# Statistics on ScalarE, a slab in halves and two more transforms by eight in a gated convolution kernel

## The chip, the cores and the metric

The kernel runs on one core of a Trainium2 chip. The metric is the device time of one execution in microseconds; before the change it is 1929.6 us, the median of three runs (1929.02 to 1932.13). A core has a matrix engine (TensorE, PE in the profile, with its weight loads as PEld), a vector engine (VectorE, DVE), an engine for functions of one operand (ScalarE, ACT), a general engine (GpSimd, POOL) and a queue engine (SyncE, SP). Each of them works through its own instructions in order and waits on semaphores for the others. SP, ACT and POOL also issue DMA transfers between the memory (HBM) and the core's own memory; TensorE writes its products into the banks of a small memory, PSUM, from which ScalarE and VectorE read.

## The reference

The reference computes a forward pass and all gradients of a block with two branches, for a sequence of S = 2048 rows and D = 1024 columns in bf16:

```python
xn = layernorm(x)                       # x = A_q
k_shift = causal convolution of k with 4 taps per column (A_shift_k)
kv = k_shift * v
y = irfft(rfft(kv, padded to 2S) * rfft(ssm_k, padded to 2S))[:S] + kv * ssm_D
s = xn * y
g = silu(((xn @ w_gate) * (xn @ w_up)) @ w_down)     # F = 3584
out = x + s * g
```

The outputs are out and the gradients of x, k, v, shift_k, ssm_k, ssm_D, w_gate, w_up and w_down, taken with a given grad_out.

## The kernel before

The rows are 16 blocks of 128. The first stage normalises them, turns them (transposes them 128 by 128 on TensorE) into the tiles XNT, and multiplies them with the gate and up weights. The weights come in 14 slabs of 256 columns of F. One unit (`gu_unit`, L629) takes one slab and 1, 2 or 4 blocks: for each block eight matmuls of 128x512 into a bank psg (L645, two banks), a cast to gut on ScalarE (L647) and a store of gut. The product of gate and up, hN, is one multiply on VectorE for the whole unit (L659). It is written one block later, into the order of the next unit. Five blocks after that TensorE turns hN (L674), ScalarE copies it, and it is stored for the down product.

The layer norm (`layer_norm`, L554) works on chunks of 1, 1, 2, 4, 4 and 4 blocks. For each block VectorE takes two `bn_stats` and a `bn_aggr`; for the chunk it casts the variances to var_b, adds epsilon (vpe, L566), ScalarE takes the root (half_r, L569), VectorE forms the reciprocal and normalises block by block (L580). The order of the loads on SP is: chunk 0, chunk 1, slab 0, chunk 2, slab 1, chunks 3 to 5 (L866 to L872).

The convolution (`conv_forward`, L685) works on eight groups of 128 columns, with Fourier transforms that are split: TensorE multiplies with small tables T4 (psF, L235), ScalarE copies the sums out (SP), and VectorE adds and subtracts them into the spectra. KX and HX are the spectra of the filter and of kv; `product` multiplies them; the inverse (`inv_dft` or `inv8` on VectorE, then psY on TensorE) gives y. Each transform has two forms. One does a split by four on VectorE (`fwd4_sums` and `fwd4_outs`, `inv_dft`) and leaves more matmuls; the other does a split by eight (`fwd8`, L297; `inv8`, L395) with half the matmuls and more VectorE instructions. The list `EIGHT` names the pairs of group and transform that take the second form, and `INV8` the groups whose inverse does. The shifted product of k with the taps (`shift`, L703) starts the convolution and comes again for every second group; it is not to start before the last normalisation (`last`, L710).

The order of convolution work beside the units is set by a pump: each block of a unit is a tick (`tick`, L918), and at each tick the pump emits convolution work until its share, in weights that stand at the yields, has come up to the share of ticks over `NT`. From the first transform on VectorE's instructions are pinned to the written order (`PIN`), and on each engine the order is fixed when the program is built. Before that point the order comes from a scheduler; `issue_after` keeps an instruction from being placed before another. The start of the stage also has: the turning of the last two chunks, put off to a later unit (`turn_late`, L602); the angles of the tables, made on POOL, masked on VectorE and turned into sines on ScalarE (L169 to L184); the first loads of k, v and the filter (A_ssm_k, into U5) on POOL.

After the units comes the down product (psbm, L971), with the gate and the gradients behind it. These later stages are not touched.

## Time and profile before

| what | us |
|---|---|
| median of three runs | 1929.6 |
| profiled execution | 1929.84 |
| its span, first to last instruction | 1928.1 |
| TensorE busy | 1914.2 |
| VectorE busy | 1542.1 |
| ScalarE busy | 638.8 |
| first forward convolution multiply on VectorE | 51.30 |
| first psbm matmul on TensorE | 519.0 |

The profiled execution's own time holds 1.7 us around the span. A line of a timeline gives the start, the length, engine, line, operation, tile written and read, shapes and count, and in brackets the idle time of the engine before it with what ended it. A line of waits gives the engine and tile that waited, for what, the sum, the number of times and the longest, in microseconds. A busy TensorE is not one at its peak, since the ends of its matmuls are modelled; the granted clock says how fast it ran.

### The profile page before, as it was taken

How to read it: one execution, taken by the hardware profiler on the slowest of the kernel's cores; microseconds unless marked ns; L12 is line 12 of the kernel's file. 1: busy time of each engine (PE TensorE's matmuls, PEld its weight loads, DVE VectorE, ACT ScalarE, POOL GpSimd, SP SyncE). 2: the span in 40 equal slices, each digit the busy share in tenths (PEclk: the TensorE clock that was granted, in tenths of full speed). 3: DMA queues.
4: the chain of work that ended last, by engine and by line, in shares of the span. 5: the costliest groups of instructions: out<-in, count | busy, mean ns of one | idle time of the engine just before them, and what ended most of it. 6: DMA issues, size and time to landing. Idle time of an engine off the chain costs nothing.

```text
span 1928.1 us, 27453 instructions
## 1 busy us (share of the span) xinstructions
PE 1914.2 (99%) x10978; PEld 1030.8 (53%) x10978; DVE 1542.1 (80%) x1695; ACT 638.8 (33%) x943; POOL 329.1 (17%) x461
## 2 busy tenths in 40 slices
PE   8999999999999999999999999999999999999999
PEld 5555655555444456665666666664444444444444
DVE  8999999999956555888799999999996403388884
ACT  5754655555332233343222222222222102011113
POOL 5121212201112210000122132021211101111111
PEclk9999999999999999999999999999999999999999
DMA  8776867659799988666788798585787999889984
GB/s 292 269 259 217 261 208 236 219 209 293 242 294 293 302 284 262 208 202 215 253 249 262 245 244 264 200 273 177 223 254 175 152 199 201 177 174 200 187 189 159
DMA packets 451360, 444.43 MB, mean 231 GB/s; under 512 B 268800, under 2 KB 371612, under 8 KB 436768
## 3 DMA queue, kind: packets, MB, share of 16 engines
q1 hardware_dynamic: 394848, 243.36, 47.7%
q0 software_dynamic: 40064, 169.95, 28.0%
q10 hardware_dynamic: 16320, 29.36, 4.1%
q8 instruction: 86, 1.41, 0.3%
q14 instruction: 42, 0.34, 0.1%
HBM read 194.00 MB, written 185.64 MB: 197 GB/s over the span
## 4 chain that ended last, share of the span: by engine, by line
PE 91%; DVE 6%; issue 1%; ACT 1%; DMA 0%; SPq 0%; ACTq 0%; DVEq 0%
PE psb L1344 20%; PE psx L1474 20%; PE psg L645 14%; PE psb L1327 10%; PE psbm L971 10%; PE psb L1422 9%; PE psF L235 3%; DVE W L213 2%; DVE HX L213 1%; PE tr L674 1%; PE psY L438 1%; DVE KX L213 1%; PE psY L1130 1%; PE psx L1422 1%; DVE U L213 1%
## 5 line engine op out<-in xcount | busy, mean ns | idle before, releaser
L645 PE MATMUL psg<-wslab,U 128*128 128x512 bf16 x1792 | 408.9, 380 | 3.4 <-DMA wslab<-in_B_w_gate_dram 2.5
L1344 PE MATMUL psb<-U,U 128*128 128x512 bf16 x1792 | 397.1, 379 | 0.0
L1474 PE MATMUL psx<-U,dgut 128*128 128x512 bf16 x1536 | 332.8, 379 | 0.0
L1474 PEld LDWEIGHTS <-dgut 128*128 128x128 bf16 x1792 | 175.1, 98 | 211.6
L1344 PEld LDWEIGHTS <-U 128*128 128x128 bf16 x1792 | 175.1, 98 | 198.1
L645 PEld LDWEIGHTS <-U 128*128 128x128 bf16 x1792 | 172.6, 98 | 189.0 <-issue 3.9
L1327 PE MATMUL psb<-wdt,U 128*128 128x256 bf16 x1792 | 205.6, 273 | 0.0
L1327 PEld LDWEIGHTS <-U 128*128 128x128 bf16 x1792 | 175.1, 98 | 29.4
L1422 PE MATMUL psb<-U,U 128*128 128x512 bf16 x816 | 177.1, 379 | 0.0
L213 DVE TENSOR_TENSOR W<-W 128x1024 f32<-128x1024 f32 (+1 forms) x174 | 171.5, 1002 | 3.7
L1349 ACT CAST wb<-psb 128x512 bf16<-128x512 f32 x112 | 65.6, 586 | 315.1 <-PE psb L1344 310.5
L971 PE MATMUL psbm<-U,ht 128*128 128x512 bf16 x672 | 145.7, 379 | 0.0
L1422 PEld LDWEIGHTS <-U 128*128 128x128 bf16 x896 | 87.4, 98 | 104.6
L647 ACT CAST gut<-psg 128x512 bf16<-128x512 f32 x156 | 91.4, 587 | 123.8 <-PE psg L645 123.4
L1506 ACT ACTIVATE dx_t<-dxn 128x1024 bf16<-128x1024 f32 x15 | 15.9, 1057 | 324.4 <-DVE dxn L213 324.4
L1182 DVE SCALAR_TENSOR_TENSOR dkp<-dkT,kT 128x1024 bf16<-128x1024 bf16 (+2 forms) x64 | 78.3, 1224 | 36.9 <-DMA dkT<-DKSHd 34.9
L971 PEld LDWEIGHTS <-ht 128*128 128x128 bf16 x672 | 65.5, 98 | 78.7
L213 DVE TENSOR_TENSOR U<-U,dht 128x2048 bf16<-128x2048 bf16 x56 | 68.3, 1220 | 45.7 <-ACT dht L1329 45.6
L1329 ACT CAST dht<-psb 128x512 bf16<-128x512 f32 x112 | 65.6, 587 | 116.4 <-PE psb L1327 116.4
L66 POOL DMA_DIRECT2D Hd<-hN x54 | 37.2, 688 | 296.3 <-DVE hN L213 294.1
L213 DVE TENSOR_TENSOR dxn<-psx,dxna_t 128x1024 f32<-128x1024 f32 x15 | 18.3, 1222 | 80.0 <-PE psx L1474 76.1
L1453 ACT CAST wbs<-psb 128x512 bf16<-128x512 f32 x51 | 29.9, 586 | 145.3 <-PE psb L1422 137.2
(237 smaller groups left out, 2451.5 us busy)
## 6 DMA issues: line engine op xcount, KB each, us to landing
U<-GUd SPq DMA_DIRECT2D x28, 1024.0 KB, 7.3
DGd<-U SPq DMA_DIRECT2D x28, 1024.0 KB, 6.4
GUd<-gut ACTq DMA_DIRECT2D x39, 512.0 KB, 6.1
out_dram<-wb SPq DMA_DIRECT2D x112, 128.0 KB, 4.3
U<-Hd SPq DMA_DIRECT2D x14, 1024.0 KB, 6.1
Hd<-hN POOLq DMA_DIRECT2D x54, 256.0 KB, 4.5
HTd<-hT SPq DMA_DIRECT2D x52, 256.0 KB, 3.7
ht<-HTd SPq DMA_DIRECT2D x6, 1536.0 KB, 9.7
```

The costliest lines, as they stand in the source:

```text
L213: pinned(V.tensor_tensor(o, a, b, op))
L235: mm = nc.tensor.matmul(ps[:, k].rearrange("p (c d) -> p c d", c=2), T[:, r, k, :], xr[:, r], start=(n == 0), stop=(n == len(rs) - 1 and ( ...
L645: gu_mm[0] = nc.tensor.matmul(ps[:], XNT[q][:, dc, qi * P:(qi + 1) * P], w[:, dc].rearrange("p a f -> p (a f)"), start=(dc == 0), stop=(dc ...
L647: nc.scalar.copy(out=gut[:, :, i], in_=ps[:].rearrange("p (a f) -> p a f", a=2))
L971: mm = nc.tensor.matmul(ps[:, dh * 512:(dh + 1) * 512], ht(fc)[:, i * P:(i + 1) * P], WD[fc // 4][:, fc % 4, dh * 512:(dh + 1) * 512], sta ...
L1182: ins = V.scalar_tensor_tensor(prod[:].rearrange("p r d -> p (r d)")[:, lo:H], dkT[:, 0, lo:H], 1.0, kT[:, 0, 13 + m + lo:13 + m + H], op0 ...
L1327: nc.tensor.matmul(ps[:, x * SLW:(x + 1) * SLW], DBMT[2 * hf + g][:, dc, (b % 4) * P:(b % 4 + 1) * P], wdt[:, dc, :], start=(dc == 0), sto ...
L1329: nc.scalar.copy(out=dht[:, 2 * e:2 * e + 2].rearrange("p b f -> p (b f)"), in_=ps[:])
L1344: nc.tensor.matmul(ps[:], XN[b // 4][:, b % 4, dc * P:(dc + 1) * P], dgus[b // 8][:, :, b % 8], start=(b == 0), stop=(b == NB - 1))
L1349: nc.scalar.copy(out=wb[:, dc % 2].rearrange("p a f -> p (a f)"), in_=ps[:])
L1422: nc.tensor.matmul(ps, h[:, f, b, :], DBM[b // 4][:, b % 4, dh * 512:(dh + 1) * 512], start=(b == 0), stop=(b == NB - 1))
L1474: nc.tensor.matmul(ps[:, dh * 512:(dh + 1) * 512], t[n][:, f, i * P:(i + 1) * P], WGU[n][:, f, dh * 512:(dh + 1) * 512], start=(n == 0 and ...
```

## The change

- The first slab is loaded in two halves of its rows, with chunk 1 between them on SP.
- In each of the three chunks of four blocks, the statistics of the last block are taken by ScalarE: a pass with a sum, a pass of squares about the mean with a sum, and three scalings. They are held behind an earlier ScalarE instruction (`hold`).
- Group 4's filter transform joins `EIGHT` and group 0's inverse joins `INV8`. `NT` goes from 209 to 213.
- The unit of chunk 5 on slab 0 moves behind the start of the pump and gets ticks; the last turnings are called ahead of it.
- The first filter load loses the condition that kept it behind a store of chunk 3. The first loads of k and v move from chunk 3 to chunk 2's place.
- The first product of the first shift gets the condition that its first multiply has.

```diff
-    def load_slab(sl, eng):
-        w = fw.tile([P, DC, 2, SLW], BF16, name="wslab")
+    def load_slab(sl, eng, part=None, w=None):
+        if w is None:
+            w = fw.tile([P, DC, 2, SLW], BF16, name="wslab")
         fs = slice(sl * SLW, (sl + 1) * SLW)
+        if part is not None:
+            cs_, rs_ = slice(4 * part, 4 * part + 4), slice(512 * part, 512 * part + 512)
+            for a, wsrc in ((0, B_w_up), (1, B_w_gate)):
+                last = eng.dma_start(out=w[:, cs_, a, :], in_=wsrc[rs_, fs].rearrange("(dc p) f -> p dc f", p=P))
+            return w, last
...
-        for i in range(n):
+        var_b = small("var_b", BF16)
+        own_ = n - {4: 1, 8: 1, 12: 1}.get(b0, 0)
+        hold = {4: act_copy[0], 8: roots.get(4), 12: copies.get(4)}.get(b0)
+        for i in range(own_, n):
+            junk = lnp.tile([P, D], BF16, name="junk")
+            s1, s2, negm = [lns.tile([P, 1], F32, name=nm_) for nm_ in ("s1", "s2", "negm")]
+            with tc.issue_after(hold.ins):
+                nc.scalar.activation(junk[:], x4[:, i, :], ACT.Identity, accum_out=s1[:])
+            nc.scalar.activation(negm[:], s1[:], ACT.Copy, scale=-1.0 / D)
+            nc.scalar.activation(mv[:, i, 0:1], s1[:], ACT.Copy, scale=1.0 / D)
+            nc.scalar.activation(junk[:], x4[:, i, :], ACT.Square, bias=negm[:], accum_out=s2[:])
+            nc.scalar.activation(var_b[:, i:i + 1], s2[:], ACT.Copy, scale=1.0 / D)
+        for i in range(own_):
             bst = lns.tile([P, 2, 6], F32, name="bst")
...
-        var_b = small("var_b", BF16)
-        V.tensor_copy(var_b, mv[:, :, 1])
+        V.tensor_copy(var_b[:, 0:own_], mv[:, 0:own_, 1])
...
+        roots[b0], copies[b0] = root, act_copy[0]
...
-    EIGHT = ((0, 0), (0, 1), (7, 0), (7, 1))
-    INV8 = (2, 4, 6)
+    EIGHT = ((0, 0), (0, 1), (4, 0), (7, 0), (7, 1))
+    INV8 = (0, 2, 4, 6)
...
             for j in (2, 1, 0):
-                tt(prod, k[:, :, 3 - j:11 - j, :], wb(j), MUL)
+                with tc.issue_after(last.ins) if dp == 0 else nullcontext():
+                    tt(prod, k[:, :, 3 - j:11 - j, :], wb(j), MUL)
...
-        with tc.issue_after(xsts[3].ins):
-            load_h(0)
+        load_h(0)
...
-    for c in xs[0:2]:
-        ln_load(*c)
-    slabs = [load_slab(0, nc.sync)[0]]
+    ln_load(*xs[0])
+    slabs = [load_slab(0, nc.sync, 0)[0]]
+    ln_load(*xs[1])
+    load_slab(0, nc.sync, 1, slabs[0])
...
-        if i == 3:
-            with tc.issue_after(xsts[4].ins):
                 for _ in range(2):
                     next(conv)
...
-        for i_, sl in ([(0, 0)], [(1, 0), (0, 1), (1, 1)], [(2, 0), (2, 1)], [(3, 0), (3, 1)], [(4, 0)], [(5, 0)])[i]:
+        for i_, sl in ([(0, 0)], [(1, 0), (0, 1), (1, 1)], [(2, 0), (2, 1)], [(3, 0), (3, 1)], [(4, 0)], [])[i]:
             gu_unit(sl, *xs[i_][0:2], slabs[sl], nop)
-        if i == len(xs) - 1:
-            with tc.issue_after(root.ins), tc.issue_after(last.ins):
-                mask_angles(ang)
-                build_tables(tg, ang)
+    with tc.issue_after(root.ins), tc.issue_after(last.ins):
+        mask_angles(ang)
+        build_tables(tg, ang)
...
+    turn_late()
     ps_st.release()
...
-    NT = 24 * 8.0 + 17
+    NT = 24 * 8.0 + 21
...
     pump((SHIFT_W + 3.95) / F_TOTAL)
+    gu_unit(0, *xs[5][0:2], slabs[0], tick)
```

More of the change, by code (lines that the diff above doesn't have):

```diff
@@ L552, in build_kernel @@
     turn_rows = []
+    roots, copies = {}, {}
     def layer_norm(b0, n, x4):
```

## The prediction

> **What bounds the kernel now.** I read the page first, then who waits for whom, then the stretch around the one long wait.

> ```profile
> span 1928.1 us, 27453 instructions
> PE 1914.2 (99%) x10978; PEld 1030.8 (53%) x10978; DVE 1542.1 (80%) x1695; ACT 638.8 (33%) x943; POOL 329.1 (17%) x461
> PE   8999999999999999999999999999999999999999
> DVE  8999999999956555888799999999996403388884
> ```

> TensorE is busy all through, so fewer matmuls look like time saved. But in slices 2 to 11 VectorE has its nines too. Those are the slices with the forward convolution beside the gate/up products. The windows view puts numbers on it (stretch and its length, then busy time of PE, PEld, DVE, ACT, POOL, clock, DMA share, GB/s):

> ```profile
> 20.20:43.40 23.20, 20.91 (x152) 11.39 (x150) 22.09 (x60) 15.02 (x26) 14.44 (x20) 1.00 0.81 283
> 72.92:489.20 416.28, 412.57 (x2580) 231.45 (x2579) 411.93 (x375) 237.62 (x333) 69.76 (x99) 1.00 0.72 235
> 485.00:488.00 3.00, 0.23 (x2) 0.00 (x0) 2.96 (x5) 0.00 (x0) 0.00 (x0) 1.00 0.85 244
> 488.00:491.50 3.50, 3.30 (x14) 1.75 (x15) 3.46 (x5) 1.50 (x2) 1.23 (x2) 0.51 1.06 407
> ```

> From 72.92 to 489.20 VectorE stands still for 4.4 us in 416. The waits of TensorE (all, longest) and of VectorE between 51 and 534 us:

> ```profile
> PE tr L674 <- DVE hN L213: 3.0, 1, 3.0
> PE psg L645 <- DMA wslab<-in_B_w_gate_dram: 2.5, 2, 1.5
> ...
> DVE hN L213 <- ACT gut L647: 3.9, 2, 3.3
> DVE W L213 <- ACT SP L295: 2.1, 1, 2.1
> DVE U L213 <- DMA k<-in_A_k_dram: 0.5, 1, 0.5
> ```

> The longest wait of TensorE is for a VectorE multiply hN that stands behind convolution work:

> ```profile
> 488.20 1.04 PE L674 MATMUL tr<-ident,hN 128*128 128x128 bf16 x8 [2.96 <-DVE hN L213]
> 489.02 5.04 PE L645 MATMUL psg<-wslab,U 128*128 128x512 bf16 x17
> ...
> 422.02 4.62 DVE L213 TENSOR_TENSOR W<-SP 128x1024 f32<-128x1024 f32 x4
> 426.56 4.62 DVE L213 TENSOR_TENSOR KX<-W 128x1024 bf16<-128x1024 f32 x4
> 431.29 4.63 DVE L213 TENSOR_TENSOR W<-SP 128x1024 f32<-128x1024 f32 x4
> ```

> After the 2.96 us wait the granted clock is 0.51 for 3.5 us; 17 matmuls there take 5.04 us. So this stage is already set by both engines, with VectorE three microseconds too slow at one place. Call that place the tight multiply: it ends at 488.15 before. The first psbm matmul starts at 519.0, 30.85 us later. From there on the two builds have the same instructions in the same order on every engine, so the change is worth exactly what it moves that matmul by.

> **The change part by part.**

> *Transforms by eight, TensorE.* A forward half is 16 matmuls in 1.75 us (L235 x16) and becomes 8 in 0.87; two halves save 1.75. The inverse is four times 8 matmuls (L449, 0.87) and becomes four times 4 (L438, 0.44), 1.74 less. Together -3.5 us.

> *The same on VectorE.* A forward transform without the split lasts from 422.02 to 431.29, 9.3 us. One by eight (the filter of block 7) lasts from 472.32 to 489.38, 17.06 less two hN multiplies of 0.60, 15.9: +6.6. The inverse costs 9.4 (524.05 to 533.45) and by eight 15.8 (455.29 to 472.32 less two multiplies): +6.4. Together +13.0 us, on an engine with 4.4 us free in 416.

> *Balance at the tight multiply.* I added the VectorE work from the end of the last normalisation (46.5) to the tight multiply, row by row at start-to-start durations: 437.3 us. The trace has 441.65; the difference is 4.3 us of waits (1.1 and 0.6 for gate casts, 0.5 for k, 2.1 for SP). In the changed order that work is 447.65: +13.0, less 2.65 that comes after the tight multiply because the convolution is spread over 213 ticks instead of 209. The 4.3 us of waits I cost at nothing: VectorE is later than what it waits for; if that cover is wrong, up to 4.3 comes on top. TensorE from its first moved unit to the transposes of the tight multiply: 437.3 before (47.9 to 485.2) and 433.4 after, so it would arrive at 481.3. VectorE arrives 447.65 after its last normalisation, at 494.1 if that ends when it did. So TensorE waits, in several places from 80 us on, and the 3.5 us saved are lost in waiting. Behind the tight multiply TensorE has 0.4 us more to do, with the same loss of clock. Sum of this part: 447.65 - 441.65 + 0.4 = **+6.4 us**, plus whatever the last normalisation moves by.

> *Statistics of three blocks on ScalarE.* VectorE drops three times 1.3 us (two bn_stats and an aggregate; four blocks take 18.91 to 24.2), -3.9. ScalarE gets per block two passes over 1024 columns (1.06 us each, as the pass with a sum at L1506), two reads of the accumulator (0.19) and three column instructions (0.2, as half_r): 3.1, together 9.3. These stand in ScalarE's order between the casts of psg that free TensorE's banks and the copies of turned blocks. The square root of the last chunk (half_r, 43.42) now stands behind two more casts, one hT copy and the Dz scaling: 1.16 + 0.57 + 1.04. So ScalarE has 15.0 + 9.3 + 2.8 = 27.1 us to do from 20.2 on, where 23.2 were available. It reaches half_r at 47.3; or at 45.2 if the added 22 instructions overlap by 0.1 each, as neighbours do in the trace. Stepping through the order with TensorE's waits for casts I get 46.3, +2.9, and take that. The step adds a wait: vpe on VectorE now needs the variance from ScalarE, and behind it stand the normalisation, the angle masks and the whole convolution, so TensorE waits in the end. The floor, if all of it were hidden, is VectorE's own -3.9.

> *First slab in halves, x1 behind the first half.* The first matmul can start when block 0 is turned (8.7) instead of at 9.9. But the next stop is the second slab, whose landing ends the second DMA wait (1.5 us, at 15.31), and as many bytes lie ahead of it as before. What TensorE gains it waits there: 0. x1 then has 0.5 MB more ahead of it, some 1.8 us at the 285 GB/s of that stretch; its statistics start at 6.9 and x0 landed at 3.4, so it is just in time. Two more issues on SP (0.4 us each) lie beside the transfers.

> *Filter load without its wait.* The 512 KB load of A_ssm_k now goes out on POOL behind the first XNd store, near 8 us instead of 34. The eight k and v loads move up by some 10 us on POOL, past Hd and XNd stores that nobody waits for; Wbc's wait for WTd holds POOL as before. The DMA share from 2 to 24 us is about 1, so at 350 GB/s the filter load can push the second slab by 0 (it fits in gaps) to 1.5 us (all of it ahead). Slab and ScalarE's 20.2 move together; I take the middle, +0.7. [...]

> *Moved to after the start:* the unit of the last chunk on slab 0, its transposes and their copies. The work is the same and lies in a stretch that waits for VectorE: 0. The first product of the convolution may no longer precede the last normalisation; it did not before (51.3 against 46.5): 0.

> Sum: 2.9 + 0.7 + 6.4 = +10.0 us on 1929.84, the profiled execution's own time, 0.24 above the median. **1939.6 us.**

> **The rivals.**
> - *ScalarE has room.* It idles 8.2 us in the 23.2, and if the added passes filled that, VectorE's -3.9 would stand: -3.9 + 0.7 + 6.4 = +3.2, 1932.8. Against it: the passes stand in order between casts that TensorE needs.
> - *VectorE keeps up and TensorE sets the end.* Then its 3.5 us, the 2.96 us wait and 1.15 us of lost clock are gained: -7.6, 1922.0. The place is the tight multiply, and it decides if VectorE is there by 481.3, that is if the last normalisation ends by 33.6; no change at all needs 40.1. Before, the chunk ahead of it is only normalised from 35.1 on.
> - *A slower start.* Slab late by 1.5, no overlap on ScalarE and 1 us of waits: half_r at 49.8, +6.4 + 6.4 = +12.8, 1942.4.

> **How the numbers follow.** A measurement tells no change from 0.2%, 3.9 us. Chances: forecast 0.62 (own range 1936 to 1942), ScalarE has room 0.17, VectorE keeps up 0.08, slower start 0.13. Slower by over 0.2%: 0.62 + 0.13 and half of the second, 0.83. Within: the other half, 0.09. Faster: 0.08. The range leaves out the third case and the tail of the fourth: from 1932, under the second, to 1943.5.

> **What would show it.** Right: the largest wait of TensorE is tr for hN, 12 to 18 us in all between 80 and 495, with 5 us or more in one piece near 490; VectorE without idle time from 53 to 535; half_r of the last chunk at 46 to 48; first psbm matmul near 529; last forward VectorE work near 543. Wrong: half_r before 44 (second case), no wait for hN (third), or the second slab later than 17 us with ScalarE idle behind it. The forecast falls if VectorE's added operations take less than the rows that I borrowed, or if the order of the build is not what runs.

## The result and the profile after

The changed kernel takes 1943.8 us (median of four runs, 1942.5 to 1945.3) against 1929.3 us of the kernel before on the same chip: 1.0073 times as long, with a 95% interval of 1.0058 to 1.0089. The forecast was 1939.6; 1943.8 lies 0.3 us above the upper end of its range, and its sign was right. The profiled execution took 1942.5 us, 12.7 more than that of before; it is one of the two shorter of the four, which stand in two pairs (1942.5 twice, 1945.1 and 1945.3), and no trace of a longer one is at hand. Its page begins like this (busy time of each engine, then the share of VectorE in 40 slices):

```profile
span 1940.7 us, 27289 instructions
PE 1908.8 (98%) x10811; PEld 1031.0 (53%) x10946; DVE 1551.4 (80%) x1708; ACT 645.9 (33%) x964; POOL 330.2 (17%) x461
DVE  6999999999957554888899899999996403488873
```

TensorE is busy for 5.4 us less than before, VectorE for 9.3 us more, and the span is 12.6 us longer: the engine that looked like the bound on the page got less to do, and the time went up. The windows view of the kernel after, in the two long stretches that were shown of before and in two short ones (columns as there, the granted clock behind the brackets of POOL):

```profile
20.20:43.40 23.20, 21.41 (x160) 12.18 (x161) 19.87 (x51) 21.83 (x44) 11.99 (x16) 0.99 0.82 269
72.92:489.20 416.28, 407.82 (x2496) 228.17 (x2542) 412.49 (x381) 234.77 (x332) 70.02 (x99) 1.00 0.70 234
...
498.30:505.20 6.90, 5.95 (x21) 2.65 (x22) 6.83 (x10) 1.78 (x3) 1.25 (x2) 0.51 0.83 295
17.00:20.50 3.50, 3.50 (x17) 1.88 (x16) 0.92 (x3) 0.59 (x1) 3.28 (x4) 0.51 1.02 419
```

In the first row ScalarE has gone from 15.0 to 21.8 us of 23.2. In the second TensorE stands for 8.5 us of the 416 (before 3.7), while VectorE works on. In the last two the clock is half: once behind the tight multiply, as before but for longer, and once near 17 us, which before did not have. Who TensorE waited for (all, number, longest):

```profile
PE tr L693 <- DVE hN L213: 4.7, 1, 4.7
PE psF L235 <- DVE kv L213: 3.0, 2, 1.6
PE psg L664 <- DMA wslab<-in_B_w_gate_dram: 2.3, 2, 2.0
PE psF L235 <- ACT SP L257: 1.8, 2, 0.9
```

VectorE's only wait between 51 and 534 us is this one, of the same view:

```profile
DVE hN L213 <- ACT gut L666: 2.5, 1, 2.5
```

The timeline of the kernel after has the places where the time comes in:

```profile
16.35 3.33 PE L664 MATMUL psg<-wslab,U 128*128 128x512 bf16 x9 [1.98 <-DMA wslab<-in_B_w_gate_dram]
...
47.59 0.17 DVE L584 TENSOR_SCALAR vpe<-var_b 128x4 bf16<-128x4 bf16 x1 [3.31 <-ACT var_b L576]
49.08 0.18 DVE L590 RECIPROCAL rec<-half_r 128x4 f32<-128x4 f32 x1 [1.33 <-ACT half_r L587]
...
499.25 1.03 PE L693 MATMUL tr<-ident,hN 128*128 128x128 bf16 x8 [4.73 <-DVE hN L213]
500.08 6.79 PE L664 MATMUL psg<-wslab,U 128*128 128x512 bf16 x18
```

The account between these places (before, after, difference, what the forecast had). A cast and half_r count from their start; the tight multiply is taken at the start of the transposes of its product on TensorE, some 0.05 us after it ends:

| from | to | before us | after us | difference | forecast |
|---|---|---|---|---|---|
| start | ScalarE's cast ahead of the statistics | 20.22 | 22.56 | +2.34 | +0.7 |
| that cast | half_r of the last chunk | 23.20 | 26.29 | +3.09 | +2.9 |
| half_r | end of the last normalisation | 3.14 | 2.97 | -0.17 | 0 |
| last normalisation | tight multiply | 441.64 | 447.43 | +5.79 | +6.0 |
| tight multiply | first psbm matmul | 30.81 | 32.56 | +1.75 | +0.4 |
| first psbm matmul | end of the span | 1409.1 | 1408.9 | -0.2 | 0 |

The first five differences add up to 12.8 us, the shift of the first psbm matmul (519.01 to 531.81). VectorE's work and ScalarE's statistics came out within 0.2 us of the forecast. What was missed lies in the first row and the fifth, and most of it is lost clock. A time in the start of one trace is good to about a microsecond only: five kernels whose start is that of before (before, b_plus_eight, b_nt213, b_eight_nt217, b_eight_less71_nt214 below) end the last normalisation between 45.43 and 46.56, and the trace of before is the latest of them.

### The profile page after: what moved, and what is told of

Its sections match the earlier page's. It is cut to its first block, busy times and chain, and to the rows that moved or that the text cites. A ratio compares the mean times of both kernels' runs of the same rounds, so it can differ in the third digit from the quotient of the medians.

```text
span 1940.7 us, 27289 instructions
## 1 busy us (share of the span) xinstructions
PE 1908.8 (98%) x10811; PEld 1031.0 (53%) x10946; DVE 1551.4 (80%) x1708; ACT 645.9 (33%) x964; POOL 330.2 (17%) x461
## 4 chain that ended last, share of the span: by engine, by line
PE 78%; DVE 14%; issue 3%; ACT 1%; DVEq 0%; ACTq 0%
PE psb L1363 20%; PE psx L1493 20%; PE psb L1346 10%; PE psbm L990 10%; PE psb L1441 9%; PE psg L664 5%; DVE W L213 5%; DVE HX L213 2%; DVE KX L213 2%; DVE U L213 2%; DVE m L213 1%; DVE hN L213 1%; PE psF L235 1%; PE psY L438 1%; PE psY L1149 1%
## 5 line engine op out<-in xcount | busy, mean ns | idle before, releaser
L664 PEld LDWEIGHTS <-U 128*128 128x128 bf16 x1792 | 173.4, 98 | 192.1 <-issue 10.1
L213 DVE TENSOR_TENSOR W<-W 128x1024 f32<-128x1024 f32 (+1 forms) x183 | 180.3, 1002 | 4.0
L1525 ACT ACTIVATE dx_t<-dxn 128x1024 bf16<-128x1024 f32 x15 | 15.9, 1057 | 326.6 <-DVE dxn L213 322.7
L213 DVE TENSOR_TENSOR U<-U,dht 128x2048 bf16<-128x2048 bf16 x56 | 68.3, 1221 | 47.3 <-ACT dht L1348 47.2
L213 DVE TENSOR_TENSOR dxn<-psx,dxna_t 128x1024 f32<-128x1024 f32 x15 | 18.3, 1222 | 83.2 <-PE psx L1493 80.2
```

Source lines behind the costliest of these rows:

```text
L213: pinned(V.tensor_tensor(o, a, b, op))
L664: gu_mm[0] = nc.tensor.matmul(ps[:], XNT[q][:, dc, qi * P:(qi + 1) * P], w[:, dc].rearrange("p a f -> p (a f)"), start=(dc == 0), stop=(dc ...
```

## The experiments

Kernels whose names begin with a are the kernel after with one thing taken back; those with b are the kernel before with one thing added. "Tight multiply" is, as in the prediction, the multiply hN for whose product TensorE waits last before the first psbm matmul. Where a difference between two changed kernels is named, it is that of their medians; each ratio is that to the kernel before on the same chip.

| kernel | median us | ratio, 95% interval | end of the last normalisation | first psbm matmul |
|---|---|---|---|---|
| before (profiled) | | | 46.56 | 519.01 |
| after | 1943.82 | 1.0073 [1.0058, 1.0089] | 51.82 | 531.81 |
| a_less_eight | 1933.72 | 1.0025 [1.0012, 1.0038] | 50.39 | 520.65 |
| a_less_stats | 1940.03 | 1.0052 [1.0035, 1.0068] | 50.74 | 531.19 |
| a_late_filter | 1939.11 | 1.0046 [1.0028, 1.0064] | 49.28 | 527.74 |
| a_whole_slab | 1942.94 | 1.0063 [1.0045, 1.0082] | 50.68 | 530.19 |
| b_plus_eight | 1936.42 | 1.0032 [1.0022, 1.0042] | 45.43 | 524.97 |
| b_plus_stats | 1929.96 | 0.9997 [0.9987, 1.0006] | 49.03 | 518.83 |
| b_plus_both | 1938.55 | 1.0053 [1.0030, 1.0076] | 48.77 | 527.55 |
| b_plus_filter | 1932.06 | 1.0009 [1.0000, 1.0018] | 49.67 | 520.67 |
| b_nt213 | 1928.09 | 1.0011 [0.9985, 1.0036] | 45.44 | 513.50 |
| b_eight_nt217 | 1931.44 | 1.0012 [0.9999, 1.0024] | 45.86 | 514.03 |
| b_eight_less71_nt214 | 1923.21 | 0.9965 [0.9951, 0.9978] | 46.33 | 512.30 |

**The transforms by eight, taken back.**

```diff
-    EIGHT = ((0, 0), (0, 1), (4, 0), (7, 0), (7, 1))
-    INV8 = (0, 2, 4, 6)
+    EIGHT = ((0, 0), (0, 1), (7, 0), (7, 1))
+    INV8 = (2, 4, 6)
```

> The kernel after, with the two added transforms by eight taken back (EIGHT and INV8 as before; NT stays 213). Theory (VectorE's work from the last normalisation sets the tight multiply): 13.0 us of VectorE's work go, TensorE gets 3.5 us back. With the convolution spread over 213 ticks, VectorE is then several microseconds ahead near 490, and TensorE only waits once near 66 us, for kv, 4 to 6 us, because of the later start. The first psbm matmul comes 8 to 9 us earlier than the 531.8 of the kernel after, near 523; time 1934, between 1932 and 1936. Rival (the later start costs everything, the transforms are neutral): 1942 to 1944, psbm near 531. Rival (TensorE sets the end): TensorE's 3.5 us come on top, 1946.

Measured 1933.7 us, 10.1 under the kernel after. The first rival falls: without the transforms, and with a last normalisation that ends only 1.43 us earlier, 4.5 us of the loss are left. So does the second: TensorE has 3.5 us more to do and the kernel is faster. The wait for hN, in the waits of TensorE in this kernel, is all but gone:

```profile
PE tr L693 <- DVE hN L213: 0.4, 1, 0.4
```

The one wait near 66 us came as three of 0.8 to 1.6 us between 58 and 67, for hx and a cast, not for kv. The first psbm matmul came 11.2 us earlier, not 8 to 9: the tight multiply moved by 8.27, and behind it the clock is not half at all, which gives the other 2.9. This execution is the shortest of its ten.

**The statistics, taken back.**

```diff
-        own_ = n - {4: 1, 8: 1, 12: 1}.get(b0, 0)
+        own_ = n
```

> The kernel after, with all statistics on VectorE again (own_ = n). Theory: half_r of the last chunk loses the 3.1 us that ScalarE's added work costs and stands near 45 (43.4 before, plus the later second slab and its half clock); every microsecond at the last normalisation counts fully, so the first psbm matmul comes 3 to 4 us earlier than 531.8, near 528.5; time 1939, between 1938 and 1940.5. Rival (TensorE's and VectorE's waits take up the start's delay, and only the transforms by eight cost): 1942 to 1944, unchanged. Rival (ScalarE had room, and VectorE's 3.9 us return): half_r later than in the kernel after, 1944 or more.

Measured 1940.0, 3.8 us under the kernel after and between the theory's ends; the two intervals overlap by little, and the trace does not confirm the gain (first psbm matmul 0.6 us earlier, not 3 to 4). The trace is of the second longest of its five executions (1941.9). Its second slab came late, and the clock fell to half for 6.83 us, so half_r stands at 47.8 and not near 45:

```profile
17.07 4.00 PE L664 MATMUL psg<-wslab,U 128*128 128x512 bf16 x9 [3.11 <-DMA wslab<-in_B_w_gate_dram]
```

Counted from the cast at 24.45, half_r comes after 23.32 us, 2.97 sooner than in the kernel after. So the price of the statistics is seen in this stretch; what it is worth at the end rests on the medians.

**The filter load, held back again.**

```diff
-        load_h(0)
+        with tc.issue_after(xsts[3].ins):
+            load_h(0)
```

> The kernel after, with the first filter load held behind the fourth XNd store again. Theory (the 512 KB of the filter, in front of the second slab's tail, delay it): the second slab's products start at 15.3 instead of 16.35, no stretch of half clock at 17 us, half_r near 46.5 instead of 48.85, the first psbm matmul 2 to 2.5 us earlier; time 1940.3, between 1939.5 and 1941. Rival (the order of the first slab's halves and of chunk 1, or the two more transfers, delay the second slab): start stays at 16.35, time unchanged, 1942 to 1944.

Measured 1939.1, 4.7 us under the kernel after and 0.4 below the theory's range. In the timeline of this kernel the wait ahead of the second slab's products is 0.83 us instead of 1.98, and the nine matmuls take 2.10 us, not 3.33:

```profile
15.11 2.10 PE L664 MATMUL psg<-wslab,U 128*128 128x512 bf16 x9 [0.83 <-ACT half_r L587]
```

The line names half_r, but the wait is still for the slab: its last load lands at 14.98, 0.13 us ahead of these matmuls, and in the kernel after at 16.21, 0.14 ahead. half_r of the last chunk is at 46.32 and the last normalisation ends 2.54 us earlier than in the kernel after; the tight multiply follows by 2.52 (499.25 to 496.73). The other 1.6 us of the 4.07 by which the first psbm matmul moved come from the clock: behind the tight multiply it is half for 3.41 us, not for 6.83. So the early load cost 1.6 us more than its own delay. The load leaves POOL at 51.46 in this kernel, and not near 34 as before, behind the loads of k and v; those were not moved back here.

**The first slab in one piece.**

```diff
-    ln_load(*xs[0])
-    slabs = [load_slab(0, nc.sync, 0)[0]]
-    ln_load(*xs[1])
-    load_slab(0, nc.sync, 1, slabs[0])
+    for c in xs[0:2]:
+        ln_load(*c)
+    slabs = [load_slab(0, nc.sync)[0]]
```

> The kernel after, with the first slab loaded in one piece behind chunks 0 and 1 again. Theory (the halves are worth nothing, and the filter load delays the second slab): the first product moves back to 9.9, the second slab's products stay at 16.2 to 16.6, time unchanged within 1 us, 1942 to 1944. Rival (the halves delay the second slab): its products start at 15.3, half_r 2 us earlier, 1940 to 1941. Rival (the halves are a gain that another part hides): later by up to 1.5 us, 1944 to 1945.

Measured 1942.9, which can't be told from the kernel after. The first product starts at 9.24 instead of 8.29, and the second slab's at 16.51:

```profile
16.51 2.10 PE L664 MATMUL psg<-wslab,U 128*128 128x512 bf16 x9 [2.80 <-DMA wslab<-in_B_w_gate_dram]
```

What TensorE gains with the halves it waits for the second slab, and the late slab is the filter load's doing.

**One part alone, on the kernel before.** The edits are those of the change:

```diff
--- b_plus_eight
+    EIGHT = ((0, 0), (0, 1), (4, 0), (7, 0), (7, 1))
+    INV8 = (0, 2, 4, 6)
--- b_plus_stats
+        own_ = n - {4: 1, 8: 1, 12: 1}.get(b0, 0)
...
--- b_plus_filter
-        with tc.issue_after(xsts[3].ins):
-            load_h(0)
+        load_h(0)
```

> The kernel before, with only the two transforms by eight added (EIGHT and INV8 as after; NT stays 209). Theory (VectorE sets the tight multiply): the start is that of before, TensorE waits in several places for VectorE, 13 to 15 us in all with 4 to 6.5 us in one piece near 490; the first psbm matmul comes 7 to 8 us later than 519.0, near 527; time 1937.5, between 1936 and 1939. Rival (the later start costs everything): 1929, unchanged. Rival (TensorE sets the end): 3.5 us less, 1926.

> The kernel before, with only the statistics of three blocks on ScalarE. Theory: from the cast at 20.2 to half_r of the last chunk takes 26.3 us, as in four traces that have these statistics, against 23.2 before: half_r near 46.5, and all behind it 3.1 us later; time 1932.3, between 1931.3 and 1933.3. Rival (VectorE's 3.9 us return): 1925.5. Rival (the delay is taken up by TensorE's and VectorE's waits before 485): 1929 to 1930.

> The kernel before, with only the first filter load sent early, as in the kernel after. Theory: the second slab's products start 0.9 to 1.8 us later than 15.3, in part of the executions at half clock; TensorE's and VectorE's delay of up to 3 us both stay inside the wait of 2.96 us at the tight multiply and VectorE's own 4.3 us: time 1929.5 to 1931.5. Rival (the filter load costs the same 4.7 us that it gave back when it was taken out of the kernel after): 1933 to 1935. Rival (the load fits in gaps of the DMA traffic): slab at 15.3, 1929.5.

The transforms alone cost 6.9 us (1936.4), as expected. The way there was a little shorter than expected: TensorE's gaps over 0.6 us between 50 and 500 us add up to 12.1 us instead of 13 to 15, the longest is 3.0 instead of 4 to 6.5, and the first psbm matmul comes 6.0 later instead of 7 to 8. Most of the waits of b_plus_eight are not for hN:

```profile
PE psF L235 <- DVE kv L213: 5.7, 3, 2.4
PE tr L674 <- DVE hN L213: 3.0, 1, 3.0
PE psF L235 <- ACT SP L257: 1.9, 2, 1.6
```

The statistics alone cost nothing that can be measured (1930.0), though half_r is 2.5 us later (3.1 were expected): the theory of that run failed, and its second rival held. The timeline of VectorE in b_plus_stats shows where the delay went:

```profile
48.95 0.67 DVE L213 TENSOR_TENSOR hN<-gut 128x1024 bf16<-128x1024 bf16 x1
49.55 1.21 DVE L213 CUSTOM_DVE_ANT_0 mm<-m,mm 128x2048 uint16<-128x2048 uint16 x1
...
52.05 2.27 DVE L213 TENSOR_TENSOR U<-k,Wbc 128x4096 bf16<-128x4096 bf16 x1
```

Before, VectorE waits 1.09 us for the cast that this hN reads and 0.49 for k ahead of the multiply U<-k,Wbc, at 51.30. Here the last normalisation ends 2.47 us later and both waits are gone, so the multiply is only 0.75 later; the wait for SP (2.10 to 1.76) and one of 0.59 for a cast at 240 us take the rest. TensorE gets its hN at 488.27, against 488.20 before.

The filter load alone costs 2.6 us (1932.1), half a microsecond above what the theory allowed. It does not slip into VectorE's waits: TensorE and ScalarE, for which VectorE waits, are late as well, so the waits move along (2.82 us for SP, up to 76.17). The last normalisation ends 3.11 us later and the tight multiply comes 3.24 later. TensorE, which in b_plus_stats is done with its work ahead of the tight multiply at 485.23, as before (485.24), is done with it at 488.49 here. TensorE's wait there stays:

```profile
491.44 0.62 PE L674 MATMUL tr<-ident,hN 128*128 128x128 bf16 x8 [2.95 <-DVE hN L213]
491.90 3.83 PE L645 MATMUL psg<-wslab,U 128*128 128x512 bf16 x17
```

17 matmuls take 3.83 us here against 5.04 before: the clock stays full behind a wait of the same length, and the first psbm matmul is only 1.66 us later.

**Two parts together.**

```diff
     (b_plus_stats, and)
+    EIGHT = ((0, 0), (0, 1), (4, 0), (7, 0), (7, 1))
+    INV8 = (0, 2, 4, 6)
```

> The kernel before, with the two transforms by eight and the statistics on ScalarE together (NT 209). Theory, formed after the statistics alone cost nothing (1929.96): VectorE has 4.3 us of waits of its own that take up the first 4.3 us of any delay; the statistics alone stay inside them, the transforms by eight use them up, so the same statistics must now count nearly in full: half_r near 46, first psbm 2.5 to 3 us later than the 524.97 of the transforms alone, time 1939.2, between 1938 and 1940.5. Rival (the statistics cost nothing in any case): 1936 to 1937, as the transforms alone (1936.4).

Measured 1938.6, 2.1 us above the transforms alone; the intervals of the two overlap, the traces differ by 2.58 us at the first psbm matmul. It is the size that was expected, but not all by the way that was expected. The last normalisation ends 3.34 us later than with the transforms alone. VectorE idles 2.1 us less before the tight multiply, which comes only 0.90 later (497.24 to 498.14). The rest is clock: it is half for 3.41 us behind this wait of 2.37, and it was not behind the one of 3.01. The 17 matmuls behind it, with the transforms alone and with both:

```profile
497.91 3.83 PE L645 MATMUL psg<-wslab,U 128*128 128x512 bf16 x17
498.81 5.52 PE L658 MATMUL psg<-wslab,U 128*128 128x512 bf16 x17
```

**The order of the work, not its amount.**

```diff
--- b_nt213
-    NT = 24 * 8.0 + 17
+    NT = 24 * 8.0 + 21
--- b_eight_nt217
     (the lists of the kernel after, and)
+    NT = 24 * 8.0 + 25
--- b_eight_less71_nt214
+    EIGHT = ((0, 0), (0, 1), (4, 0), (7, 0))
+    INV8 = (0, 2, 4, 6)
+    NT = 24 * 8.0 + 22
```

> The kernel before, with only NT changed from 209 to 213. Theory: the convolution is spread further behind the tight multiply, VectorE is there before TensorE, and the wait of 2.96 us with the 1.15 us of lost clock behind it goes; no wait for hN over 0.7 us; first psbm matmul near 515, time 1924.8, between 1924 and 1926. Rival (the work that is pushed back makes TensorE wait later, for HX or yf near 540): 1927 to 1930.

> The kernel before, with the two transforms by eight and NT at 217. Theory (the added work costs by where it stands, ahead of the tight multiply or behind it): some 10 us of VectorE's work move behind the tight multiply, the wait there falls to 2 to 3 us, and one of about 3 us appears near 539 for the last HX; time 1928.5, between 1926 and 1931. Rival (13 us of VectorE's work cost the same wherever they stand): 1936 to 1939.

> The kernel before, with group 4's filter transform and group 0's inverse by eight, but group 7's second transform, which stands right ahead of the tight multiply, by four, and NT at 214. Theory (what counts is VectorE's work ahead of the tight multiply, not the number of splits): VectorE has 6.2 us more in all, but more of it behind the tight multiply; TensorE has 1.7 us less; no wait for hN over 0.7 us, first psbm near 513, time 1924, between 1922.5 and 1926.5. Rival (any added transform by eight costs its 6.4 us less the 4.3 us of waits): 1931 to 1933.

With NT at 213 alone the profiled execution does what was expected: no wait of TensorE over 0.6 us between 50 and 500 us, first psbm matmul at 513.5, 1924.3 us. But its ten runs spread from 1924.3 to 1946.7 with a median of 1928.1, so a gain is not shown, and no trace of one of the longer ones is at hand. The cause of that spread stays open.

With both transforms added and NT at 217, the loss shrinks from 6.9 to 1.9 us (1931.4, 0.4 above the expected range; the profiled execution took 1929.5), and its interval reaches down to no loss. The wait for the tight multiply is 0.4 us instead of the 2 to 3 expected; the expected one behind the first psbm matmul is there:

```profile
542.98 1.01 PE L449 MATMUL psY<-HX,TI 128*128 128x256 bf16 x4 [2.89 <-DVE HX L213]
```

So the same 13 us of VectorE's work cost 6.9 us with NT at 209, 1.9 with 217 and, between a_less_eight and the kernel after, which have the late start and NT at 213, 10.1. What they cost goes by where the work stands and by the waits that are left to take it up. The 1.9 is counted from the kernel before with its NT of 209; from the one profiled execution with NT at 213 alone (1924.3) it would be 5.2.

The last kernel keeps the two added transforms, drops the one by eight that stands right ahead of the tight multiply (group 7, second form), and spreads over 214. It takes 1923.2 us, 0.9965 [0.9951, 0.9978] of the kernel before: faster than both. TensorE has no gap over 0.6 us between 50 and 500 us; the stretch that held the long wait is now full (windows view, TensorE first):

```profile
485.00:488.00 3.00, 2.95 (x15) 1.35 (x15) 3.00 (x6) 1.17 (x2) 0.00 (x0) 1.00 0.79 236
488.00:492.00 4.00, 4.00 (x29) 2.55 (x28) 4.00 (x4) 1.72 (x3) 0.69 (x1) 1.00 0.34 121
```

VectorE is busy 5.4 us longer than before (1547.5 us), and TensorE has 1.7 us less to do by the prediction's rows. How much of the 6.3 us comes from the spread alone is not shown: the shortest execution of b_nt213, which spreads over 213 and adds no transform, is nearly as fast (1924.3, first psbm matmul 1.2 us later), and the original lists at NT 214 were not tried.

## Why the prediction was nearly right, and where it was not

- *Balance at the tight multiply, +6.0.* Right: +5.79. The row-by-row sum (447.65 us from the last normalisation to the tight multiply) met 447.43. "The 4.3 us of waits I cost at nothing" is borne out by the trace, in which VectorE waits for nothing between 51 us and the tight multiply: its idle time in that stretch falls from 8.2 to 4.1 us. What is left are gaps of under 0.15 us between its instructions, and they correct a reading of the prediction: of the "4.4 us free in 416" before, 3.8 were such gaps, which the kernel after has too, and only 0.6 a wait. Most of the cushion lay ahead of that stretch, in waits that ended at 50.11, 51.30 and 72.92 us.
- *Statistics, +2.9.* Right in the sum: +3.09 from the cast to half_r, a stretch of 26.29 to 26.31 us in six traces. But the price holds only in company. Alone the statistics cost nothing (b_plus_stats): the 4.3 us of VectorE's waits can be used up once, by the statistics or by the transforms, and the prediction's sum gives them to the transforms.
- *Filter load, +0.7.* This is the step that failed. The slab came 1.04 us later, inside the bounds of 0 and 1.5, but "slab and ScalarE's 20.2 move together" was wrong: the wait of 1.98 us cost a stretch of half clock, the nine matmuls behind it took 3.33 us instead of 2.10, and the cast was 2.34 us late. With the filter load early the second slab's products start at 16.22 to 17.07 (five traces), without it at 14.24 to 15.31 (eight): 1.8 us apart in the mean, and 1.2 between the kernel after and a_late_filter, so the price is nearer to the upper bound of 1.5, or above it, than to the middle that was taken. With that bound in its place the prediction's sum would have been 0.8 higher. The landings agree with it: in the five traces the filter load leaves 1.7 to 2.4 us after the slab's last load and lands 0.2 to 2.0 us ahead of it, so all of it has landed before the slab has.
- *Behind the tight multiply, +0.4 "with the same loss of clock".* Also wrong in size: +1.75, since the longer wait (4.73 us against 2.96) left the clock at half for 6.83 us, not 3.41. In a_late_filter, with the same work and one stretch of 3.41 us, this row takes 31.01 us, 1.55 less than in the kernel after.
- *TensorE's -3.5 us lost in waiting.* Right in the way, and less than foretold: its gaps over 0.6 us add up to 9.6 us from 80 us on, where 12 to 18 were foretold, with 3.7 more between 58 and 68; the longest is 4.7 instead of 5 or more. They were foretold mostly as waits for hN; only those 4.7 us are. TensorE meets VectorE's lateness at psF too, where it waits for kv or for ScalarE's copies of SP.
- *Halves and moved unit, 0.* The halves are borne out by a_whole_slab. The moved unit and the earlier loads of k and v were not tried alone.
- *The signs foretold.* The second slab not later than 17: 16.35. VectorE without idle time: one wait of 2.5 us, at 510. half_r at 46 to 48: 48.85, late by the clock. First psbm matmul near 529: 531.81. Last forward VectorE work near 543: 546.2.

Of the rivals, "VectorE keeps up" and "ScalarE has room" did not come about. "A slower start" (1942.4) is nearest in size, and right in its place; its way was another, since the slab was not later than forecast by much, and what was added was clock. Together the start (1.3, the cast's 2.34 less the slab's 1.04) and the tail (about 1.4) hold 2.7 us of lost clock that the prediction had nowhere. That is nearly all of the 2.9 us by which the profiled execution passed the forecast; the median lies 1.3 us further up, and what the longer executions lost is not shown.

## What to carry to other kernels

Where two engines are within a few microseconds of each other over a long stage, price a change on both, count the waits of the slower one as a cushion that can be spent once, and add the parts up only after that. A cushion of waits takes up a delay of the waiting engine alone; a delay that also moves what it waits for passes through in full, as the filter load's did (3.11 us at the last normalisation, 3.24 at the tight multiply). Moving work past the place where the engines meet can be worth nearly as much as removing it: of the 6.9 us that 13 us of added work cost the kernel before, 5.0 came back by a constant in the pump, and a kernel with more VectorE work in all was the fastest. Parts that share such a cushion and one wait do not add up: taken back one at a time, transforms, statistics and filter load are worth 10.1 + 3.8 + 4.7 = 18.6 us, and added one at a time 6.9 + 0.4 + 2.6 = 9.9, for a change of 14.5.
